# A hashed attention followed by a feed-forward layer: row maxima turned by a product with the identity, a step of the weight conversion one unit sooner, and two small groups of work moved

## The chip, the cores and the metric

The kernel runs on one core of a Trainium2 chip. The metric is device time in microseconds (us), the median of several executions. The engines are TensorE (PE, with its weight loads PEld), VectorE (DVE), ScalarE (ACT), GpSimd (POOL) and SyncE (SP), which issues nearly all DMA transfers. Times in rows of the trace count from the start of the profiled span.

## The reference

```python
B, H, S, D = q.shape                                  # 4, 8, 768, 64
q_bits = (einsum('bhsd,dk->bhsk', q, proj) > 0)       # 6 bits; k_bits likewise
q_bucket = sum(q_bits * powers, axis=-1)              # k_bucket likewise
mask = q_bucket[:, :, :, None] == k_bucket[:, :, None, :]
scores = where(mask, scale * q @ k.T, -1e9)
scores = scores - max(scores, axis=-1, keepdims=True)
attn = exp(scores)
attn = attn / (sum(attn, axis=-1, keepdims=True) + 1e-09)
attn_out = attn @ v
x = attn_out.transpose(0, 2, 1, 3).reshape(B * S, H * D)      # 3072 x 512
h = x @ w_in                                          # 512 x 2048
g = where(h >= 1, h, where(h <= -1, 0, (h + 1)**2 / 4))
out = g @ w_out                                       # 2048 x 512
```

## The kernel before, in words

All products run on fp32r operands split in a high and a low part, so that each product of the reference is three or so on PE. The first 457 us are the attention of 32 heads (four batches of eight), the rest is the feed-forward layer.

**Units.** The attention's order is written out by hand. A head has 12 units (`NU`): two halves of 384 queries by six blocks of 128 keys; unit g belongs to head g // 12. In unit g the code emits: two score products (`s_unit`, L369 and L370) into one of four PSUM buffers `s`; ACT's two exponentials (L378 writes `ph`, L383 writes the full-precision copy in place or to `pf`); for the unit before, the subtraction `pl` = full - `ph` (`lo_unit`, L39; on POOL for key blocks 0 and 3, else on DVE); then three products with V for the unit four before (`pv_unit`, L402, L404, L406) into the PSUM bank `o0` (first half of a head) or `o1` (second half). After the sixth of a half ACT copies the bank out (L412, `xs<-o`).

**Row maxima.** The maxima of a head are found two heads ahead, in six steps: two products (`max_mm`, L308) into `smax`, a pair of PSUM banks of which there is only one, and a reduction of both on DVE (`max_red`, L312, into `nm`). The six pairs stand at the end of units 4, 6, 8, 10, 12 and 14 of the head that runs, and each reduction in the unit behind; so a pair waits for the reduction of the pair before it. POOL then clamps the six columns and makes six flags (`max_clamp`, unit 15), PE turns the 128 x 12 block into rows (`max_tr`, L347, unit 17), ACT copies it to `te` (L352) and SP writes it by DMA into the row of ones of the query operand (`t<-te`, L354) and to DRAM (L355). Heads 0 to 2 do this in halves or otherwise (`row_half`, `half_put`).

**Weight conversion.** The weights come as 64-bit floats and are converted in 512-column pieces while the attention runs; each head from 3 to 26 carries one. The steps of a piece (`WeightSplit.steps`) stand at units counted from that head's first: DMA in (0), `rebias` on ACT (L66), and three on DVE: `tail` (L70, a shift right), `shifted` (L74, shift left and or) and `signed` (L78). `tail` and `shifted` write their word into PSUM bank `o0`, which is free between the copy of a head's first half (in unit 9) and the next head's first product with V in unit 16. `conv` places the steps by a list of units.

**Other tasks.** Tasks placed by `at(g, ...)` are emitted at the end of unit g, in the order of their placing. Every engine, and SP's queue, runs its instructions in the order in which they are emitted. For each pair of heads (`pr`), POOL makes the operands of the pair two ahead (`cast_h`, `low_h`), SP moves halves of them between partitions (`move`, L161, 384 KB each) and loads the raw pair after it (`load_raw`, L145). Even heads carry in addition two groups of products for the hash bits (`bits_mm`, end of units 5 and 7) with an ACT copy each (L214), and a cast of V on ACT (L287, unit 6). Once per batch `XMaker.sums_add` (L672, L673) and `sums_inv` (L677) turn the row sums into factors on DVE.

Of the kernel before, what the change touches and what calls it, by code (L numbers as in the profile page):

```python
# [11 lines left out]
F32 = mybir.dt.float32  # L12
F32R = mybir.dt.float32r
# [9 lines left out]
P = 128  # L23
NH = B * H
NPAIR = NH // 2
NJ = S // P
# [6 lines left out]
CLAMP = 2.0 ** 33  # L33
# [74 lines left out]
NU = 2 * NJ  # L108
# [3 lines left out]
def attention(ctx, tc, wst, T1, T2, qk, v, pj, cv, x_d, s_d, e_d, tasks, shared):  # L112
    nc = tc.nc
    const = ctx.enter_context(tc.tile_pool(name="aconst", bufs=1))
    work = ctx.enter_context(tc.tile_pool(name="awork", bufs=2))
    small = ctx.enter_context(tc.tile_pool(name="asmall", bufs=2))
# [6 lines left out]
    ident = const.tile([P, P], F32, name="ident")  # L123
    cvt = const.tile([32, 2], F32, name="cvt")
    cvd = const.tile([40, 2], F32, name="cvd")
    ident_r = const.tile([P, P], F32R, name="ident_r")
# [1 line left out]
    warm = const.tile([P, 2], F32, name="warm")  # L128
    nrow = [const.tile([P, NJ, 33], F32R, name=f"nrow{h}") for h in range(2)]
    pj_raw = const.tile([P, NB], F32, name="pj_raw")  # L130
    nmh = const.tile([P, 2, NJ], F32, name="nmh")
    pj_hi = const.tile([P, NB], F32R, name="pj_hi")
    pw = const.tile([P, 3, P], F32R, name="pw")
    VA = [const.tile([P, NJ, 3, D], F32R, name=f"va_{i}") for i in range(NV)]
# [157 lines left out]
    nms = {}  # L292
# [24 lines left out]
    HB = NJ // 2  # L317
# [8 lines left out]
    def half_put(hd, hf, bank):  # L326
        pr, h = hd // 2, hd % 2
        if hf == 1:
            nms.pop(hd)
        ps = obank[bank]  # L330
        nc.tensor.transpose(out=ps[0:2 * HB, 0:P], in_=nmh[:, hf], identity=ident)
        te = small.tile([2 * NJ, P], F32R, name="te")[0:2 * HB]
        nc.scalar.copy(out=te, in_=ps[0:2 * HB, 0:P])
        sl = slice(hf * HS, (hf + 1) * HS)
        nc.sync.dma_start(out=T2[pr % NQK][7:8, 0, h, sl].bitcast(F32), in_=te[0:HB].bitcast(F32))
        nc.sync.dma_start(out=e_d[hd // H][hd % H:hd % H + 1, sl], in_=te[HB:2 * HB].bitcast(F32))

    def max_clamp(hd, eng):
        nm = nms[hd]
        eng.tensor_scalar(out=nm[:, NJ:2 * NJ], in0=nm[:, 0:NJ], scalar1=CLAMP, scalar2=None,  # L340
                          op0=ALU.is_gt)
        eng.tensor_scalar(out=nm[:, 0:NJ], in0=nm[:, 0:NJ], scalar1=CLAMP, scalar2=None,
                          op0=ALU.min)

    def max_tr(hd, bank=None):
        ps = mx[hd] = ps_s.tile([P, 512], F32, name="s") if bank is None else obank[bank]
        nc.tensor.transpose(out=ps[0:2 * NJ, 0:P], in_=nms.pop(hd), identity=ident)  # L347

    def max_put(hd):
        pr, h = hd // 2, hd % 2  # L350
# [99 lines left out]
    def raw0():  # L450
        return wst.tile([P, DM, 2], I32, name="wraw").rearrange("p a b -> p (a b)").bitcast(F32)[:, 0:S].rearrange(
            "p (h s) -> p h s", h=1)

    def at(g, fn, *a):
        tasks[g].append((fn, a))

    first = [raw0(), raw0()]
# [92 lines left out]
    at(12, bits_put, 1)  # L550
    at(12, move, 1, 2)
    at(12, max_tr, 0, 0)
    at(12, max_put, 0)
    at(10, load_raw, 2)
# [4 lines left out]
    at(15, row_flags, 1)  # L559
    at(12, lambda: nc.gpsimd.memset(T2[2][0:64, 0].bitcast(F32), 0.0))  # L560
    at(17, max_tr, 1, 1)
    at(17, max_put, 1)
    at(18, half_clamp, 2, 0)
    at(19, half_put, 2, 0, 1)
    at(23, half_clamp, 2, 1)
    at(25, half_put, 2, 1, 0)
    for h, g in enumerate((20, 2 * NU + 1)):
        at(g, lambda h=h: nc.gpsimd.memset(T2[0][32:33, 0, h].bitcast(F32), 0.0))
    for hd in range(NH):
        pr, h = hd // 2, hd % 2  # L570
        g = hd * NU
        if 0 < hd < NH - 2:
            gc, gt = ((30, 32), (41, 43))[hd - 1] if hd < 3 else (g + NU + SHIFT - 1, g + NU + SHIFT + 1)
            at(gc, max_clamp, hd + 2, nc.gpsimd)
            at(gt, max_tr, hd + 2)
            at(gt, max_put, hd + 2)
        if h == 0 and pr + 2 < NPAIR:
            g0 = g + (13, 2)[pr] if pr < 2 else g
            for n in range(4):
                gq = g0 + n + (pr == 1 and n == 3)  # L580
                at(gq, cast_h, pr + 2, nc.gpsimd, n % 2, n // 2)
                at(gq, low_h, pr + 2, nc.gpsimd, n % 2, n // 2)
            for n in range(2):
                at(g0 + 3 + (pr == 1), move, pr + 2, n)
            at(g0 + 6, move, pr + 2, 2)
            if pr + 3 < NPAIR:
                at(g0 + 7, load_raw, pr + 3)
            bits_at = (((20, 1), (23, 0)), ((8, 1), (11, 0)))[pr] if pr < 2 else ((5, 1), (7, 1))
            for hf, (n, bank) in enumerate(bits_at):
                at(g + n, bits_mm, pr + 2, hf, bank)  # L590
                at(g + n + 1, bits_cmp, pr + 2, hf)
            at(g + n + 1, move, pr + 2, 3)
            at(g + n + (2 if pr else 1), bits_scale, pr + 2, nc.gpsimd if pr else nc.scalar)
            at(g + (18 if pr else 25), bits_put, pr + 2)
        if h == 0 and pr + 1 < NPAIR:
            gv = g + LAG + (2 if pr else 16)
            at(gv, cast_v, pr + 1, nc.scalar)
            at(gv + 1, split_v, pr + 1, nc.gpsimd, 0)
            at(gv + 3, split_v, pr + 1, nc.gpsimd, 1)
            if pr + 2 < NPAIR:  # L600
                at(gv + (6 if pr else 4), load_v, pr + 2)
# [6 lines left out]
    for i in range(2 * NJ):  # L608
        n = 5 * 31 + 35 * i // 4
# [495 lines left out]
def lsh_attn_ffn(ctx: ExitStack, tc: tile.TileContext, qk, v, pj, cv, w_in, w_out, out):  # L1105
    nc = tc.nc
# [16 lines left out]
    xm = XMaker(nc, x_d, s_d, er_d)  # L1123
# [25 lines left out]
    def at(g, fn, *a):  # L1149
        tasks[g].append((fn, a))  # L1150

    def conv(g, steps, offs):
        for fn, n in zip(steps, offs):
            at(g + n, fn)
# [6 lines left out]
    def wi_steps(i, cp, stage=None):  # L1161
        return ws.steps(win_v[:, :, i * P:(i + 1) * P, :], (P, NCT, P, 2), wih[i], wil[i], cp, stage, None, wq[i], word)

    def wo_steps(i, cp, stage=None, low=None):
        return ws.steps(wout_v[i], (P, DM, 2), woh[i], wol[i], cp, stage, low, None, None if stage is None else word)
# [1 line left out]
    woh = [hi for hi, lo in wo]  # L1167
    wol = [lo for hi, lo in wo]
    for i in range(NW1):
        conv((2 * i + 3) * NU, wi_steps(i, nc.scalar), (0, 9, 10, 12, 14, 17, 19, 21))  # L1170
    g0 = (NH - 4) * NU
    late = {}
    for n in range(NSTG):
        i = n - (NFT - NW1)
        stage = wq[NW1 + n] if i < 0 else xdp.tile([P, DM], F32, name=f"wd{n}")
        if i < 0:
            first, late[n] = wi_steps(NW1 + n, nc.vector, stage)
        elif i < 2:
            first, late[n] = wo_steps(i, nc.vector, stage)
        else:  # L1180
            first, late[n] = wo_steps(i, nc.scalar, stage, nc.gpsimd if i < 4 else nc.vector)
        conv((4 + 2 * n) * NU, first, (0, 9, 10, 12, 14, 16))
    for n, g in enumerate((1, 7, 13, 25, 30, 35)):
        conv(g0 + g, late[n], (0, 5, 6))

# [1 line left out]
    for b in range(B - 1):  # L1187
        g = (b + 1) * H * NU + LAG + 4
        at(g, lambda b=b: xm.sums_load(*(attn["small"].tile([P, NF], F32, name=n, bufs=1) for n in ("sm", "em")), b))
        at(g + 15, xm.sums_add)  # L1190
        at(g + 21, xm.sums_inv, b)
    gx = (NH - 2) * NU

    def load_raw():
# [16 lines left out]
    for i in (2, 3):  # L1211
        at(NH * NU + 2 * i - 10, late[i + NFT - NW1][0])
    attention(actx, tc, wst, T1, T2, qk, v, pj, cv, x_d, s_d, e_d, tasks, attn)
    actx.close()

# [5 lines left out]
    for i in range(2, NFT):  # L1221
        n = i + NFT - NW1
# [71 lines left out]
```

## Time and profile before

| | |
|---|---|
| median of 3 runs | 975.26 us (974.24 to 975.34) |
| profiled execution | 975.34 us, span 973.5 us, granted clock 1.000 |
| PE busy | 961.6 us (99%), 5050 products |
| PEld / DVE / ACT / POOL busy | 890.4 / 755.5 / 680.0 / 318.6 us |
| chain that ended last | PE 89%, DVE 4%, DMA 2%, ACT 2% |

The profiled execution is 1.84 us longer than its span; that part lies outside the first and last instruction. A busy PE means products in its pipeline: in the rows a product of 384 columns lasts 0.34 us while the next one starts 0.17 to 0.18 us behind it, so waits are read from starts and not from busy time.

### The profile page before, as it was taken

What the parts mean: (1) busy time and instruction counts of PE and PEld (TensorE: products, weight loads), DVE (VectorE), ACT (ScalarE), POOL (GpSimd) and SP (SyncE); (2) the same over time, 40 slices, a digit from 0 to 9 for tenths busy, and PEclk for the clock granted to TensorE, in tenths of its full rate; (3) what the DMA queues carried; (4) which work ended last, traced back from release to release, by engine and by line L of the source; (5) the groups of instructions that cost most, each with busy time, mean ns of one, the idle gap of its engine ahead of it and who ended that gap; (6) DMA issues with size and microseconds to landing.
All of it is one profiled execution on the core that took longest, in us unless ns stands there. A gap on an engine that the chain in (4) does not pass through costs nothing.

```text
span 973.5 us, 15576 instructions
## 1 busy us (share of the span) xinstructions
PE 961.6 (99%) x5050; PEld 890.4 (91%) x5050; DVE 755.5 (78%) x1323; ACT 680.0 (70%) x1481; POOL 318.6 (33%) x423
## 2 busy tenths in 40 slices
PE   8999999999999999999999999999999999999998
PEld 7899999999999999999989998888998888888886
DVE  8778888888888888896988787787876777655554
ACT  7889998999999998987656565455464545544444
POOL 8767776666677776466000000000000000000000
PEclk9999999999999999999999999999999999999999
DMA  5776565667666656535692578976458564454431
GB/s 163 190 185 180 150 171 167 179 181 200 183 195 168 163 158 182 142 104 147 187 337 88 158 227 287 294 245 199 120 171 230 147 182 117 148 154 119 117 90 65
DMA packets 95112, 167.55 MB, mean 172 GB/s; under 512 B 13956, under 2 KB 51960, under 8 KB 95032
## 3 DMA queue, kind: packets, MB, share of 16 engines
q1 hardware_dynamic: 94808, 166.56, 59.9%
q8 instruction: 40, 0.66, 0.3%
q14 instruction: 40, 0.33, 0.1%
q10 hardware_dynamic: 224, 0.00, 0.0%
HBM read 106.13 MB, written 33.87 MB: 144 GB/s over the span
## 4 chain that ended last, share of the span: by engine, by line
PE 89%; DVE 4%; DMA 2%; ACT 2%; issue 1%; SPq 1%; POOL 1%; DVEq 0%; ACTq 0%; POOLq 0%
PE y L828 27%; PE h L1060 18%; PE h L965 7%; PE smax L308 7%; PE o L406 6%; PE o L402 6%; PE s L370 6%; PE o L404 6%; PE s L369 6%; PE o L208 2%; DVE nm L312 2%; DVE pl L39 1%; DMA t<-te 1%; DMA t<-bits 1%; ACT ph L378 1%
## 5 line engine op out<-in xcount | busy, mean ns | idle before, releaser
L378 ACT ACTIVATE ph<-s 128x384 fp32r<-128x384 f32 x380 | 189.8, 499 | 40.1 <-PE s L370 33.9
L312 DVE TENSOR_REDUCE nm<-smax 128x1 f32<-128x768 f32 x189 | 180.0, 952 | 27.2 <-PE smax L308 26.9
L39 POOL TENSOR_TENSOR pl<-pf,ph 128x384 fp32r<-128x384 f32 x128 | 130.6, 1021 | 89.7 <-ACT pf L383 89.5
L39 DVE TENSOR_TENSOR pl<-s,ph 128x384 fp32r<-128x384 f32 x256 | 138.0, 549 | 26.0 <-ACT s L383 22.7
L793 DVE SCALAR_TENSOR_TENSOR t<-t 128x384 f32<-128x384 f32 x128 | 71.3, 557 | 106.3 <-ACT z L788 106.2
L369 PE MATMUL s<-t 128*128 128x384 f32 x384 | 131.1, 342 | 0.0
L406 PE MATMUL o<-pl,va 128*128 128x386 f32 x384 | 130.1, 339 | 0.9 <-DVE pl L39 0.9
L402 PE MATMUL o<-ph,va 128*128 128x386 f32 x384 | 130.0, 339 | 0.4 <-DVE wsq L78 0.4
L370 PE MATMUL s<-t 128*128 128x384 f32 x384 | 129.6, 337 | 0.5 <-DMA t<-te 0.5
L404 PE MATMUL o<-ph,vb 128*128 128x386 f32 x384 | 130.0, 339 | 0.0
L383 ACT ACTIVATE s<-s 128x384 f32<-128x384 f32 x252 | 126.2, 501 | 0.0
L828 PE MATMUL y<-t,ghi 128*128 128x512 f32 x384 | 124.6, 395 | 0.0
L308 PE MATMUL smax<-t 128*128 128x384 f32 x378 | 100.7, 347 | 3.6 <-DVE nm L312 2.9
L787 ACT ACTIVATE t<-h,mh 128x384 f32<-128x384 f32 x56 | 32.5, 581 | 83.3 <-PE h L965 44.1
L798 ACT CAST ghi<-z 128x384 fp32r<-128x384 f32 x129 | 65.1, 505 | 30.4 <-DVE z L794 26.6
L788 ACT ACTIVATE z<-t,m 128x384 f32<-128x384 f32 x128 | 79.0, 617 | 4.2
L828 PEld LDWEIGHTS y<-t,ghi 128*128 128x128 f32 x384 | 71.3, 188 | 11.1 <-ACT ghi L798 0.3
L1060 PE MATMUL h<-wbig,t 128*128 128x384 f32 x399 | 81.4, 336 | 0.0
L308 PEld LDWEIGHTS smax<-t 128*128 128x128 f32 x378 | 66.2, 188 | 14.9 <-DVE nm L312 13.8
L787 ACT ACTIVATE t<-wsq,mh 128x384 f32<-128x384 f32 x48 | 29.6, 617 | 67.0 <-DVE wsq L1073 40.7
L1060 PEld LDWEIGHTS h<-wbig,t 128*128 128x128 f32 x399 | 71.6, 188 | 5.3
L828 PE MATMUL y<-t,glo 128*128 128x512 f32 x192 | 76.0, 396 | 0.0
(192 smaller groups left out, 2074.2 us busy)
## 6 DMA issues: line engine op xcount, KB each, us to landing
t<-wc SPq DMA_DIRECT2D x92, 256.0 KB
t<-t SPq DMA_DIRECT2D x60, 384.0 KB
wraw<-wc SPq DMA_DIRECT2D x76, 256.0 KB
raw<-in_qk_dram SPq DMA_DIRECT2D x14, 768.0 KB
wraw<-in_w_in_dram SPq DMA_DIRECT2D x16, 512.0 KB
wraw<-in_w_out_dram SPq DMA_DIRECT2D x16, 512.0 KB
t<-ed SPq DMA_DIRECT2D x36, 192.0 KB
xd<-xs SPq DMA_DIRECT2D x32, 192.5 KB
```

The costliest lines, as they stand in the source:

```text
L39: eng.tensor_tensor(out=out, in0=a, in1=b, op=ALU.subtract)
L308: nc.tensor.matmul(out=smax[hd][:, hf, 0:HS], lhsT=t2[:, 0, h, i * P:(i + 1) * P], rhs=t2[:, 1, h, hf * HS:(hf + 1) * HS], start=True, sto ...
L312: nc.vector.tensor_reduce(out=nmp(hd)[:, i:i + 1], in_=smax[hd][:, :, 0:HS], axis=AX.XY, op=ALU.max, negate=True)
L369: nc.tensor.matmul(out=ps[:, 0:HS], lhsT=t1[:, 1, h, ks], rhs=t1[:, 0, h, sl], start=True, stop=False)
L370: nc.tensor.matmul(out=ps[:, 0:HS], lhsT=t2[:, 1, h, ks], rhs=t2[:, 0, h, sl], start=False, stop=True)
L378: nc.scalar.activation(out=ph[:, 0:HS], in_=ps[:, 0:HS], func=AF.Exp, scale=SCALE)
L383: nc.scalar.activation(out=pf, in_=ps[:, 0:HS], func=AF.Exp, scale=SCALE)
L402: nc.tensor.matmul(out=o, lhsT=wa, rhs=ph, start=(jj == 0), stop=False)
L404: nc.tensor.matmul(out=o, lhsT=wb, rhs=ph, start=False, stop=False)
L406: nc.tensor.matmul(out=o, lhsT=wa, rhs=pl, start=False, stop=(jj == NJ - 1))
L828: nc.tensor.matmul(out=ys[c][m], lhsT=g_[:, m * P:(m + 1) * P], rhs=w, start=(first and k == 0), stop=(last and k == 2))
L1060: nc.tensor.matmul(out=ps, lhsT=w[:, cs], rhs=x, start=(n == 0 and s not in (2, 3, 6)), stop=(n == 5), skip_group_check=True)
```

## The change

Five edits. (1) The block of maxima is turned by an ordinary fp32r product with the fp32r identity instead of a transposition in fp32; for that the clamped maxima go to a new fp32r tile `nmr` (and `nmh` becomes fp32r). Heads 0 and 1 keep the transposition. (2) In the lists of `conv`, `rebias` goes from unit 9 to 8 and `shifted` from 12 to 11; for the first piece `signed` goes from 14 to 13. (3) For the fourth pair of heads (`pr == 1`, pair index 3) three of the four moves go from units 30, 30, 32 to 33, 33, 34, and the load of the next raw pair from 33 to 34. (4) `sums_add` goes from 15 units behind the load to 7. (5) `sums_inv` goes from 21 units behind it to 19.

```diff
-    nmh = const.tile([P, 2, NJ], F32, name="nmh")
+    nmh = const.tile([P, 2, NJ], F32R, name="nmh")
...
-        nc.tensor.transpose(out=ps[0:2 * HB, 0:P], in_=nmh[:, hf], identity=ident)
+        nc.tensor.matmul(out=ps[0:2 * HB, 0:P], lhsT=nmh[:, hf], rhs=ident_r, start=True, stop=True)
...
     def max_clamp(hd, eng):
         nm = nms[hd]
-        eng.tensor_scalar(out=nm[:, NJ:2 * NJ], in0=nm[:, 0:NJ], scalar1=CLAMP, scalar2=None,
+        t = nms[hd] = small.tile([P, 2 * NJ], F32R, name="nmr")
+        eng.tensor_scalar(out=t[:, NJ:2 * NJ], in0=nm[:, 0:NJ], scalar1=CLAMP, scalar2=None,
                           op0=ALU.is_gt)
-        eng.tensor_scalar(out=nm[:, 0:NJ], in0=nm[:, 0:NJ], scalar1=CLAMP, scalar2=None,
+        eng.tensor_scalar(out=t[:, 0:NJ], in0=nm[:, 0:NJ], scalar1=CLAMP, scalar2=None,
                           op0=ALU.min)
 
     def max_tr(hd, bank=None):
         ps = mx[hd] = ps_s.tile([P, 512], F32, name="s") if bank is None else obank[bank]
-        nc.tensor.transpose(out=ps[0:2 * NJ, 0:P], in_=nms.pop(hd), identity=ident)
+        nm = nms.pop(hd)
+        if hd < 2:
+            nc.tensor.transpose(out=ps[0:2 * NJ, 0:P], in_=nm, identity=ident)
+        else:
+            nc.tensor.matmul(out=ps[0:2 * NJ, 0:P], lhsT=nm, rhs=ident_r, start=True, stop=True)
...
             for n in range(2):
-                at(g0 + 3 + (pr == 1), move, pr + 2, n)
-            at(g0 + 6, move, pr + 2, 2)
+                at(g0 + (7 if pr == 1 else 3), move, pr + 2, n)
+            at(g0 + (8 if pr == 1 else 6), move, pr + 2, 2)
             if pr + 3 < NPAIR:
-                at(g0 + 7, load_raw, pr + 3)
+                at(g0 + (8 if pr == 1 else 7), load_raw, pr + 3)
...
     for i in range(NW1):
-        conv((2 * i + 3) * NU, wi_steps(i, nc.scalar), (0, 9, 10, 12, 14, 17, 19, 21))
+        conv((2 * i + 3) * NU, wi_steps(i, nc.scalar), (0, 8, 10, 11, 14 - (i == 0), 17, 19, 21))
...
-        conv((4 + 2 * n) * NU, first, (0, 9, 10, 12, 14, 16))
+        conv((4 + 2 * n) * NU, first, (0, 8, 10, 11, 14, 16))
...
-        at(g + 15, xm.sums_add)
-        at(g + 21, xm.sums_inv, b)
+        at(g + 7, xm.sums_add)
+        at(g + 19, xm.sums_inv, b)
```

How the rows move is shown at three places. In the changed kernel lines below 340 keep their numbers, and those of `s_unit`, `pv_unit` and the te copies are five higher (L378 becomes L383, L383 becomes L388, L412 becomes L417, L354 becomes L359).

ACT in units 8 to 10 of an even head (head 6; `o_137` is bank `o0`), before:

```order
L378 ACTIVATE ph_161<-s 128x384
L383 ACTIVATE s<-s 128x384
L378 ACTIVATE ph_155<-s 128x384
L383 ACTIVATE pf<-s 128x384
L412 COPY xs<-o_137 128x384
L66 ACTIVATE wsq<-wraw 128x512
L378 ACTIVATE ph_156<-s 128x384
L383 ACTIVATE s<-s 128x384
```

and now:

```order
L383 ACTIVATE ph_161<-s 128x384
L388 ACTIVATE s<-s 128x384
L66 ACTIVATE wsq<-wraw 128x512
L383 ACTIVATE ph_155<-s 128x384
L388 ACTIVATE pf<-s 128x384
L417 COPY xs<-o_137 128x384
L383 ACTIVATE ph_156<-s 128x384
L388 ACTIVATE s<-s 128x384
```

`rebias` (L66) now stands ahead of unit 9's two exponentials and of the copy of bank `o0`, instead of behind them.

DVE from unit 9 of the same head to unit 2 of the next, before:

```order
L39 TENSOR_TENSOR pl_165<-s,ph_158 128x384
L70 TENSOR_SCALAR o_137<-wraw 128x512
L312 TENSOR_REDUCE nm<-smax 128x1
L39 TENSOR_TENSOR pl_167<-s,ph_160 128x384
L39 TENSOR_TENSOR pl_168<-s,ph_161 128x384
L74 SCALAR_TENSOR_TENSOR o_137<-wsq,wsc,o_137 128x512
L312 TENSOR_REDUCE nm<-smax 128x1
L39 TENSOR_TENSOR pl_163<-s,ph_156 128x384
L78 SCALAR_TENSOR_TENSOR wsq<-wsq,wsc,o_137 128x512
```

and now:

```order
L39 TENSOR_TENSOR pl_165<-s,ph_158 128x384
L70 TENSOR_SCALAR o_137<-wraw 128x512
L312 TENSOR_REDUCE nm<-smax 128x1
L39 TENSOR_TENSOR pl_167<-s,ph_160 128x384
L74 SCALAR_TENSOR_TENSOR o_137<-wsq,wsc,o_137 128x512
L39 TENSOR_TENSOR pl_168<-s,ph_161 128x384
L312 TENSOR_REDUCE nm<-smax 128x1
L39 TENSOR_TENSOR pl_163<-s,ph_156 128x384
L78 SCALAR_TENSOR_TENSOR wsq<-wsq,wsc,o_137 128x512
```

`shifted` (L74) has changed places with one subtraction; the same nine instructions stand ahead of and behind it.

SP's queue in units 30 to 36 (`t_1_78` is the operand that head 3 reads; `t_0_77` and `t_0_74` are being made for the fourth pair), before:

```order
L161 DMA t_0_77<-t_0_77 64x1536
L161 DMA t_0_74<-t_0_77 64x1536
L354 DMA t_1_78<-te 1x6x128
L355 DMA ed_67<-te 6x128
L161 DMA t_0_74<-t_0_74 64x1536
L145 DMA raw<-in_qk_dram 128x1536
L62 DMA wraw<-in_w_in_dram 128x4x256
```

and now:

```order
L359 DMA t_1_78<-te 1x6x128
L360 DMA ed_67<-te 6x128
L161 DMA t_0_77<-t_0_77 64x1536
L161 DMA t_0_74<-t_0_77 64x1536
L161 DMA t_0_74<-t_0_74 64x1536
L145 DMA raw<-in_qk_dram 128x1536
L62 DMA wraw<-in_w_in_dram 128x4x256
```

The two transfers of head 3's maxima now go ahead of the two moves.

## The prediction

> **What bounds the kernel now.** I read the page's busy times first, then the instructions of the maxima products with what they wait for, then single units of the attention engine by engine in the timeline.
>
> ```profile
> PE 961.6 (99%) x5050; PEld 890.4 (91%) x5050; DVE 755.5 (78%) x1323; ACT 680.0 (70%) x1481; POOL 318.6 (33%) x423
> ```
>
> ```profile
>   DVE nm L312: 16.7, 48
> ```
>
> PE is the bound over the whole span, so an edit is worth what it adds to or takes from PE's waits. The second row is from the view of line L308: PE and its weight loads sat idle 16.7 us, 48 times, ahead of a maxima product, for the reduction of the pair before it. No other releaser comes near it in the attention, and nothing in the diff touches the feed-forward part. So the question is what the edits do to that wait. On PE it looks so (a pair at the end of unit 0, then the pair of unit 2 with the product ahead of it, in head 9; then the pair of unit 2 behind the last conversion):
>
> ```profile
> 145.72 0.51 PE L308 MATMUL smax<-t 128*128 128x384 f32 x2
> ...
> 147.65 0.34 PE L406 MATMUL o<-pl,va 128*128 128x386 f32 x1
> 148.02 0.62 PE L308 MATMUL smax<-t 128*128 128x384 f32 x2
> ...
> 395.38 0.62 PE L308 MATMUL smax<-t 128*128 128x384 f32 x2
> ```
>
> An undisturbed pair takes 0.51 and starts 0.17 behind the product ahead (the steps between neighbours). At 148.02 it starts 0.37 behind and takes 0.62: a wait of 0.20 + 0.11 = 0.31 us. Behind the last piece, at 395.38, the pair takes 0.62 again. The 24 conversion pieces (heads 3 to 26) each leave one such wait in unit 2 of the next head. They come in two kinds, by whether the head that carries the piece is even or odd.
>
> **Even heads: ACT is full.** ACT, then DVE, in head 8:
>
> ```profile
> 142.09 0.49 ACT L383 ACTIVATE s<-s 128x384 f32<-128x384 f32 x1
> 142.50 0.49 ACT L378 ACTIVATE ph<-s 128x384 fp32r<-128x384 f32 x1
> ...
> 143.23 0.49 ACT L412 COPY xs<-o 128x384 f32<-128x384 f32 x1
> 143.59 0.71 ACT L66 ACTIVATE wsq<-wraw 128x512 f32<-128x512 f32 x1
> 144.17 0.51 ACT L378 ACTIVATE ph<-s 128x384 fp32r<-128x384 f32 x1
> ```
>
> ```profile
> 143.75 0.69 DVE L70 TENSOR_SCALAR o<-wraw 128x512 int32<-128x512 int32 x1
> 144.36 0.95 DVE L312 TENSOR_REDUCE nm<-smax 128x1 f32<-128x768 f32 x1
> 145.22 1.21 DVE L39 TENSOR_TENSOR pl<-s,ph 128x384 fp32r<-128x384 f32 x2
> 146.35 0.74 DVE L74 SCALAR_TENSOR_TENSOR o<-wsq,wsc,o 128x512 int32<-128x512 int32 x1
> 147.01 0.95 DVE L312 TENSOR_REDUCE nm<-smax 128x1 f32<-128x768 f32 x1
> 147.88 0.55 DVE L39 TENSOR_TENSOR pl<-s,ph 128x384 fp32r<-128x384 f32 x1
> 148.34 0.74 DVE L78 SCALAR_TENSOR_TENSOR wsq<-wsq,wsc,o 128x512 int32<-128x512 int32 x1
> ```
>
> ACT has no gap: each instruction starts before the row ahead has ended. The copy ends at 143.23 + 0.49 = 143.72 and `tail` (L70), which writes the bank that was copied, starts at 143.75. So `tail` is tied to the copy. The reduction at 147.01 ends at 147.96, and the pair of maxima starts 0.17 later.
>
> The edit puts `rebias` ahead of unit 9's exponentials and of that copy. Steps from the rows: behind L383 at 142.09 it starts 0.36 later (as 143.23 to 143.59), and the exponential 0.58 behind it (143.59 to 144.17): 143.03 instead of 142.50. The copy is late by 0.53 and `tail` starts at 144.28. From there DVE goes without a gap: reduction +0.61 (143.75 to 144.36), subtraction +0.86 (144.36 to 145.22), `shifted` +0.46 (as 147.88 to 148.34), subtraction +0.66 (146.35 to 147.01), reduction +0.46: 147.33 instead of 147.01. What it wins back of the 0.53 is the gap ahead of the second subtraction, which today waits for its exponential (two of them take 1.13 to the start of L74 where 2 x 0.46 would do) and which `shifted` now fills. Loss: 0.32 us a head. Part of it will show one pair sooner: the reduction ahead ends at 144.36 + 0.53 + 0.95 = 145.84, the pair can start at 146.01 and wanted 145.72. That 0.29 is not to be added; the wait of unit 2 shrinks by it, because DVE's row of work is not pushed by PE there. Twelve even heads (4, 6 ... 26): **+3.84 us**. Bounds: 0.53 each (nothing won back, +6.4), and a gain of 0.21 each, the whole gap won and no delay (-2.5). I take the middle value because every step in it is from a row of this stretch.
>
> **Odd heads: ACT has a gap.** Head 7, ACT, DVE and PE:
>
> ```profile
> 127.21 0.49 ACT L383 ACTIVATE s<-s 128x384 f32<-128x384 f32 x1
> 128.05 0.49 ACT L378 ACTIVATE ph<-s 128x384 fp32r<-128x384 f32 x1 [0.35 <-PE s L370]
> ```
>
> ```profile
> 129.33 0.70 DVE L70 TENSOR_SCALAR o<-wraw 128x512 int32<-128x512 int32 x1 [0.21 <-ACT xs L412]
> ...
> 132.58 0.95 DVE L312 TENSOR_REDUCE nm<-smax 128x1 f32<-128x768 f32 x1
> ```
>
> ```profile
> 133.32 0.34 PE L406 MATMUL o<-pl,va 128*128 128x386 f32 x1
> 133.59 0.62 PE L308 MATMUL smax<-t 128*128 128x384 f32 x2
> ```
>
> Here ACT waits 0.35 for PE ahead of unit 9's exponential. `rebias` falls into that gap: 127.21 + 0.36 + 0.58 = 128.15 instead of 128.05, so copy and `tail` are 0.10 late. The same chain from `tail` at 129.43 gives the reduction at 132.48 instead of 132.58. The wait of 0.10 + 0.11 = 0.21 falls by 0.10. Eight such heads (5, 7, 11, 13, 15, 19, 21, 23): **-0.8 us**; bounds 0 and -1.7 (the whole wait).
>
> **Sums of a batch.** The other odd heads, 9, 17 and 25, carry `sums_add` in the same row of DVE work:
>
> ```profile
> 156.74 0.69 DVE L70 TENSOR_SCALAR o<-wraw 128x512 int32<-128x512 int32 x1 [0.21 <-ACT xs L412]
> ...
> 158.67 0.37 DVE L672 SCALAR_TENSOR_TENSOR sm<-em,sm 128x48 f32<-128x48 f32 x1
> ...
> 160.31 0.95 DVE L312 TENSOR_REDUCE nm<-smax 128x1 f32<-128x768 f32 x1
> ```
>
> Without it, with `tail` at 156.84 and the same 3.05 of steps, the reduction comes at 159.89 instead of 160.31. That is 0.42 a head, three heads: **-1.26 us**. It now stands in unit 3 of a head, where the next reduction comes two units later, and the reciprocal too. The cover is DVE's wait for PE, seen in the reductions' group:
>
> ```profile
> L312 DVE TENSOR_REDUCE nm<-smax 128x1 f32<-128x768 f32 x189 | 180.0, 952 | 27.2 <-PE smax L308 26.9
> ```
>
> DVE idles 27.2 us ahead of 189 reductions, 0.14 each and none at units 0 and 2 in the rows above, so more elsewhere. Were that cover gone, the sums (0.52 today, 0.42 + 0.10) and a reciprocal of an estimated like size would give back up to 3 x 2 x 0.5 = 3 us; I keep this as the far end. The sums must also have landed seven units behind their load, instead of 15.
>
> **The fourth pair's moves.** In unit 36 PE waits for head 3's row of maxima. SP, ACT, then PE:
>
> ```profile
> 56.63 1.16 SPq L161 DMA_DIRECT2D t<-t  x2
> 57.88 1.21 SPq L354 DMA_DIRECT2D t<-te  x1
> ```
>
> ```profile
> 57.31 0.25 ACT L352 CAST te<-s 12x128 fp32r<-12x128 f32 x1
> ```
>
> ```profile
> 61.50 0.33 PE L369 MATMUL s<-t 128*128 128x384 f32 x1
> 62.30 0.44 PE L370 MATMUL s<-t 128*128 128x384 f32 x1 [0.47 <-DMA t<-te]
> ```
>
> The row is ready at 57.56, is issued at 57.88 behind two moves of 384 KB, and L370 starts 0.80 behind L369 instead of 0.17, and takes 0.44 instead of 0.34: 0.73 us lost. With the moves behind it the row goes first: **-0.73 us**, bounds 0 and -0.73. What is queued behind it is the moves, the raw load and the first weights: they come about 1 us later, and are wanted by PE, POOL and ACT from unit 44 on.
>
> The first piece (head 3) trades one wait for another: PE waits at
>
> ```profile
> 80.50 0.41 PE L402 MATMUL o<-ph,va 128*128 128x386 f32 x1 [0.37 <-DVE wsq L78]
> ```
>
> for `signed`, which now comes a reduction sooner, while `shifted` (0.66 of DVE) now stands ahead of the reduction that the last maxima pair of that head waits for. I count 0, from -0.5 to +0.5.
>
> **Product for transposition.** A transposition and an fp32r product of the same 128 columns (three in a row), each ahead of the score products:
>
> ```profile
> 124.07 0.27 PE L347 MATMUL s<-ident,nm 128*12 128x128 f32 x1
> 124.10 0.42 PE L369 MATMUL s<-t 128*128 128x384 f32 x1
> 124.36 0.34 PE L370 MATMUL s<-t 128*128 128x384 f32 x1
> ```
>
> ```profile
> 24.08 0.34 PE L258 MATMUL smax<-ident_r,nrow 128*33 128x128 f32 x3
> 24.26 0.39 PE L369 MATMUL s<-t 128*128 128x384 f32 x1
> 24.48 0.34 PE L370 MATMUL s<-t 128*128 128x384 f32 x1
> ```
>
> From the transposition's start to L370's it is 0.03 + 0.26 = 0.29 us; from the last of the three products 0.06 + 0.22 = 0.28. Both are some 0.11 over the 0.17 of a lone step, so the kind of product is not what costs. There are 31 (29 heads and two halves): at most 0.3 us, I take **-0.1**. The Trainium skill ("TensorE: Matmul & The Clock Gate", "LDWEIGHTS (loading the stationary operand)") gives a weight load as its columns over 1.2, 107 ns for 128. By that rule the excess is the next load, which a product this short cannot hide, and the trace's 0.11 agrees. The two clamps on POOL stay two and have two units to the product.
>
> **The sum.** 3.84 - 0.8 - 1.26 - 0.73 - 0.1 = +0.95. Against the profiled execution, 975.34 us (its span of 973.5 and 1.84 around it, 0.08 over the median of 975.26), this is 976.3 us. A measurement of this kernel can tell about 0.2%, 1.95 us, from no change: so 973.3 to 977.2 counts as the same.
>
> **Rivals.**
> - *Slower: the late copy costs in full.* In even heads the 0.53 reaches the reduction undiminished, because the second subtraction still waits for its exponential. 12 x 0.53 = 6.4, less 2.9 of the other terms: 978.8. It decides from 0.40 us a head on ((1.95 + 2.89) / 12). For it: ACT's rows have no gap. Against it: unit 10's and 11's exponentials are not moved later, and DVE reaches the subtraction later. Chance 0.28, with the smaller sizes beyond 977.2.
> - *Faster: the copy is not delayed,* and every head wins the gap on DVE: 12 x 0.21 and 8 x 0.2 off, sums 1.5, moves 0.7: 6.3 less, 969.0. It decides if the even heads lose under 0.08 each ((2.89 - 1.95) / 12). For it: only rounding of steps of ACT's stands between. Against it: ACT's order is fixed and full there. Chance 0.22, with the part gains up to 973.3.
> - *The transposition's whole length is on the path.* 0.27 against some 0.22 for the other (0.34 for three that start 0.06 apart), 31 times: 1.5 less, 974.9, still the same. The Trainium skill, section "Part 4: PE-mode transpose" of that page, reads so: about 275 ns each, and not counted as PE being busy. The length agrees with 0.27, but L369 starts 0.03 behind it and the clock stays at 1.000. Chance 0.05, within the next.
>
> **How the numbers follow.** Same, with the sum above: 0.50; slower 0.28; faster 0.22. The likeliest is 976.3, its own range 974.9 to 977.2 (odd heads and head 3 at their lower ends; above, where the case ends). For 8 in 10 the range goes down to 970.5, which leaves out the full gain of every head (1 in 10), and up to 979.0, just over the slower rival (1 in 10).
>
> **What would show it.** In the profile after, even heads should have `tail` some 0.5 us behind where it stood against the product ahead, a wait of about 0.3 at unit 0 that is not there now and about 0.3 at unit 2 still; odd heads 0.1 at unit 2; the large waits of heads 10, 18 and 26 and that of unit 36 gone; the L308 waits for L312 up by about 1 to 2 us in all. The forecast is wrong if `tail` in even heads starts as early as before, if the wait at unit 2 does not shrink by what unit 0 shows, or if a new wait for a DMA appears at unit 44 to 48 or 111.

## The result and the profile after

| | before | after |
|---|---|---|
| median of 6 runs each | 975.12 us (973.94 to 976.60) | 980.16 us (979.36 to 980.82) |
| ratio, 95% interval | | 1.0052 (1.0040 to 1.0063) |
| profiled execution / span | 975.34 / 973.5 us | 980.79 / 979.0 us |
| granted clock | 1.000 | 0.998 |

The change makes the kernel 5.0 us slower. The forecast was 976.3, so the same, with a range up to 979.0: wrong.

The page's busy times, after:

```profile
PE 965.4 (99%) x5050; PEld 891.9 (91%) x5050; DVE 754.6 (77%) x1323; ACT 680.8 (70%) x1481; POOL 317.8 (32%) x423
```

The view of line L308, PE's and PEld's idle time ahead of a maxima product and its cause:

```profile
  DVE nm L312: 18.2, 54
```

That is 1.5 us more than the 16.7 before, inside the "1 to 2" that the prediction gave, and far from 5. The rest is found by cutting both traces at the start of each unit's first score product (us; unit 383 is the last):

| units | before | after | difference |
|---|---|---|---|
| 0 to 30 | 41.01 | 40.99 | 0 |
| 30 to 36 | 8.28 | 9.59 | +1.31 |
| 36 to 48 | 13.83 | 13.09 | -0.74 |
| 48 to 60 | 14.84 | 18.17 | +3.33 |
| 60 to 324 | 302.07 | 304.15 | +2.08 |
| 324 to 383 | 61.89 | 61.39 | -0.50 |

The largest entry is head 4 (units 48 to 59). PE at its start, in the timeline (start, length, instruction, idle time and its releaser), before and then after:

```profile
75.33 0.34 PE L369 MATMUL s<-t 128*128 128x384 f32 x1
75.51 0.33 PE L370 MATMUL s<-t 128*128 128x384 f32 x1
```

```profile
75.91 0.34 PE L374 MATMUL s<-t 128*128 128x384 f32 x1
78.45 0.44 PE L375 MATMUL s<-t 128*128 128x384 f32 x1 [2.20 <-DMA t<-te]
...
79.35 0.53 PE L409 MATMUL o<-ph,vb 128*128 128x386 f32 x1
79.67 0.52 PE L411 MATMUL o<-pl,va 128*128 128x386 f32 x1
```

After the change the second score product of unit 48 waits for head 4's row of maxima: 2.36 us lost (2.54 from L374 to L375 instead of 0.17). From 79.1 the products last 0.52 instead of 0.34 and start 0.32 apart instead of 0.175. A table of stretches says why (stretch, its length, busy time and instructions of PE, PEld, DVE, ACT and POOL, then PE's granted clock, DMA share, GB/s):

```profile
72.30:75.70 3.40, 3.40 (x21) 3.40 (x20) 2.63 (x4) 2.53 (x6) 0.15 (x1) 1.00 0.98 203
75.70:79.10 3.40, 1.20 (x8) 0.88 (x7) 2.51 (x5) 1.88 (x6) 2.30 (x3) 1.00 0.31 83
79.10:82.50 3.40, 3.40 (x12) 3.40 (x11) 2.17 (x3) 1.60 (x5) 2.54 (x4) 0.50 0.38 131
```

After the stretch with the wait the clock was granted at 0.50 for 3.4 us: 12 products instead of 21, another 9 x 0.175 = 1.6 us. Together that is some 4.0; 3.33 are left in the table because the 0.7 us of waits that these units had before, for the first piece, fall away behind it.

Where the row was in the meantime is seen on ACT, which copies it, and in SP's queue:

```profile
71.84 0.25 ACT L357 CAST te<-s 12x128 fp32r<-12x128 f32 x1
```

```profile
58.86 0.74 SPq L359 DMA_DIRECT2D t<-te  x1
...
60.22 2.46 SPq L161 DMA_DIRECT2D t<-t  x3
...
67.66 0.47 SPq L161 DMA_DIRECT2D t<-t  x1
...
70.78 3.88 SPq L280 DMA_DIRECT2D t<-bits  x4
76.09 0.75 SPq L359 DMA_DIRECT2D t<-te  x1
```

It is ready at 72.09 and issued at 76.09. Before, the first move was issued at 56.63; now SP stands at head 3's row until 58.86, and the moves follow at 60.22, 3.6 us later. Before, head 4's row was issued at:

```profile
72.33 0.74 SPq L354 DMA_DIRECT2D t<-te  x1
```

Everything between has kept its order behind the moves, and is late with them. The queue's waits from 70 to 80 us name two of the causes (total, times, longest):

```profile
SPq L359 <- DMA t<-t: 1.4, 1, 1.4
SPq L280 <- DMA wraw<-in_w_in_dram: 1.1, 1, 1.1
```

The transfers of the bits stand ahead of the row and wait for the weights to land; the row then waits for a move to land, to whose data it has no relation. The program shows the reason: SP's transfers take eight completion semaphores in turn, and each waits until the one eight places ahead has landed. The row is number 58, the last move number 50:

```
50 L161 DMA t_0_74<-t_0_77 64x1536 [waits DMAHW3_49,DMAHW6_49,DMAHW1_49,PE_49]
58 L359 DMA t_2_79<-te 1x6x128 [waits DMAHW6_49,Activation_49]
```

That the DMA engines were idle until the moves came is in the DMA view from 54 to 80 us (busy tenths in 40 slices of 0.65 us; before, then after):

```profile
DMA  3920049899709996898989998999731047950000
```

```profile
DMA  3920000000079969999897978999989887310268
```

From 56 to 61 us less than a tenth is busy after the change, and the backlog ends some 3 us later.

The attention's other heads went as the prediction had them. Head 8 on ACT, DVE and PE:

```profile
146.94 0.65 ACT L66 ACTIVATE wsq<-wraw 128x512 f32<-128x512 f32 x1
...
148.23 0.48 ACT L417 COPY xs<-o 128x384 f32<-128x384 f32 x1
```

```profile
148.74 0.69 DVE L70 TENSOR_SCALAR o<-wraw 128x512 int32<-128x512 int32 x1 [0.69 <-ACT xs L417]
```

```profile
150.00 0.34 PE L411 MATMUL o<-pl,va 128*128 128x386 f32 x1
150.35 0.62 PE L308 MATMUL smax<-t 128*128 128x384 f32 x2
...
152.39 0.34 PE L411 MATMUL o<-pl,va 128*128 128x386 f32 x1
152.80 0.62 PE L308 MATMUL smax<-t 128*128 128x384 f32 x2
```

The copy (L417) ends at 148.71, and `tail` (L70) starts 1.26 ahead of unit 0's L411 where it was 1.80 ahead: 0.54 late, with an idle DVE ahead of it. The pair of unit 0 now waits (0.35 - 0.17) + 0.11 = 0.29, that of unit 2 0.24 + 0.11 = 0.35. Behind odd head 7, and behind head 9 with its sums:

```profile
137.89 0.34 PE L411 MATMUL o<-pl,va 128*128 128x386 f32 x1
138.06 0.60 PE L308 MATMUL smax<-t 128*128 128x384 f32 x2
```

```profile
165.53 0.33 PE L411 MATMUL o<-pl,va 128*128 128x386 f32 x1
165.74 0.62 PE L308 MATMUL smax<-t 128*128 128x384 f32 x2
```

0.09 and 0.15 are left of the 0.21 and 0.55 before (for head 9's sums, L406 at 160.70 and a pair of 0.62 at 161.31).

### The profile page after: what moved, and what is told of

It reads as the page before. It is cut to its first block, busy times and chain, and to the rows that moved or that the text cites. A ratio compares the mean times of both kernels' runs of the same rounds, so it can differ in the third digit from the quotient of the medians.

```text
span 979.0 us, 15556 instructions
## 1 busy us (share of the span) xinstructions
PE 965.4 (99%) x5050; PEld 891.9 (91%) x5050; DVE 754.6 (77%) x1323; ACT 680.8 (70%) x1481; POOL 317.8 (32%) x423
## 4 chain that ended last, share of the span: by engine, by line
PE 83%; DVE 8%; ACT 5%; issue 2%; DMA 2%; POOL 0%; DVEq 0%; ACTq 0%
PE y L833 27%; PE h L1065 18%; PE h L970 7%; PE smax L308 6%; PE s L375 5%; PE s L374 5%; PE o L411 5%; PE o L407 5%; PE o L409 5%; DVE nm L312 3%; DVE pl L39 2%; PE o L208 2%; ACT ph L383 2%; DVE o L70 1%; DMA t<-te 1%
## 5 line engine op out<-in xcount | busy, mean ns | idle before, releaser
L383 ACT ACTIVATE ph<-s 128x384 fp32r<-128x384 f32 x380 | 189.3, 498 | 44.2 <-PE s L375 39.8
L375 PE MATMUL s<-t 128*128 128x384 f32 x384 | 130.0, 339 | 3.7 <-DMA t<-te 3.7
L374 PE MATMUL s<-t 128*128 128x384 f32 x384 | 131.0, 341 | 0.0
L411 PE MATMUL o<-pl,va 128*128 128x386 f32 x384 | 130.4, 340 | 0.4 <-DVE pl L39 0.4
L388 ACT ACTIVATE s<-s 128x384 f32<-128x384 f32 x252 | 125.8, 499 | 0.0
L308 PE MATMUL smax<-t 128*128 128x384 f32 x378 | 102.1, 351 | 3.6 <-DVE nm L312 2.2
L308 PEld LDWEIGHTS smax<-t 128*128 128x128 f32 x378 | 65.5, 189 | 17.7 <-DVE nm L312 16.0
L375 PEld LDWEIGHTS s<-t 128*128 128x128 f32 x384 | 72.7, 189 | 4.5 <-DMA t<-te 4.3
```

What stands on the lines that cost most here:

```text
L308: nc.tensor.matmul(out=smax[hd][:, hf, 0:HS], lhsT=t2[:, 0, h, i * P:(i + 1) * P], rhs=t2[:, 1, h, hf * HS:(hf + 1) * HS], start=True, sto ...
L374: nc.tensor.matmul(out=ps[:, 0:HS], lhsT=t1[:, 1, h, ks], rhs=t1[:, 0, h, sl], start=True, stop=False)
L375: nc.tensor.matmul(out=ps[:, 0:HS], lhsT=t2[:, 1, h, ks], rhs=t2[:, 0, h, sl], start=False, stop=True)
L383: nc.scalar.activation(out=ph[:, 0:HS], in_=ps[:, 0:HS], func=AF.Exp, scale=SCALE)
L388: nc.scalar.activation(out=pf, in_=ps[:, 0:HS], func=AF.Exp, scale=SCALE)
L411: nc.tensor.matmul(out=o, lhsT=wa, rhs=pl, start=False, stop=(jj == NJ - 1))
```

## The experiments

Theory Q: the late moves hold up head 4's row, and the wait and the half clock cost some 3 us. Theory R: all of the loss comes from `rebias` one unit sooner. S: where `rebias` stands does not matter, only the place of `shifted` does. T: the transposition lay on PE's path; U: the product in its place makes head 2's row late. Each comparison has its own runs of the kernel before beside it (single ones took 973.6 to 978.7 us), so ratios are compared; a ratio can differ by 0.001 to 0.002 from the quotient of the two medians. "Half clock" below counts the runs with a mean granted clock of 0.998 or less, which is what one stretch of 3.4 us at 0.50 makes of it.

### The moves back

```diff
-                at(g0 + (7 if pr == 1 else 3), move, pr + 2, n)
-            at(g0 + (8 if pr == 1 else 6), move, pr + 2, 2)
+                at(g0 + 3 + (pr == 1), move, pr + 2, n)
+            at(g0 + 6, move, pr + 2, 2)
...
-                at(g0 + (8 if pr == 1 else 7), load_raw, pr + 3)
+                at(g0 + 7, load_raw, pr + 3)
```

> The changed kernel with the fourth pair's moves and the raw load back at units 30, 30, 32 and 33. Theory Q (the moves, put behind head 3's row, start 3 us late, so that head 4's row lands late, PE waits 2.2 us in unit 48 and then runs 3.4 us at half clock): the wait of unit 48 and the half clock go, the 0.73 us of unit 36 come back; 980.2 - 3.3 + 0.7 = 977.6 us, granted clock 1.000. Theory R (all of the loss is rebias ahead of the copy in even heads): no change, 980 us. If the 1.5 us wait of unit 30 also belongs to the moves: 976.3. If it belongs to edit 1 or to chance, it may stay.

978.89 us, ratio 1.0020 (1.0008 to 1.0031), against 1.0052 with the late moves: the edit costs about 3 us by the ratios (1.3 by the bare medians; units 48 to 60 of the two traces differ by 3.35). Those units take 14.82 us, there is no wait for a row at unit 48, and 2 of 10 runs have the half clock where all 6 after had it. Q holds in what it says of unit 48, though its total of 977.6 does not quite. Some 2 us of loss are left for R. One thing goes against the prediction's gain: the trace shows no wait at unit 36 either (36 to 48: 13.10), although the moves stand ahead of head 3's row again. That wait comes and goes.

### `rebias` back in unit 9

```diff
-(0, 8, 10, 11, 14 - (i == 0), 17, 19, 21))
+(0, 9, 10, 11, 14 - (i == 0), 17, 19, 21))
...
-(0, 8, 10, 11, 14, 16))
+(0, 9, 10, 11, 14, 16))
```

> The changed kernel with rebias back in unit 9, shifted kept in unit 11. Theory Q and my step for even heads (tail 0.53 late with rebias ahead of the copy): the waits of units 0 and 2 behind the twelve even heads (0.28 and 0.34 us in the trace) shrink to 0.1 in unit 2, those behind odd heads to nearly nothing; 980.2 - 12 x 0.53 - 11 x 0.1 = 972.7 us, with the half clock at unit 48 still there (clock 0.998). Theory R: back to before or better by the same, 972 to 975, and the clock at 1.000. Rival S (where rebias stands does not matter, shifted does): 980, waits of units 0 and 2 as they are.

972.96 us, ratio 0.9966 (0.9951 to 0.9981): this kernel is faster than the one before. `tail` on DVE, and the pairs of units 0 and 2 on PE, behind head 8:

```profile
144.55 0.69 DVE L70 TENSOR_SCALAR o<-wraw 128x512 int32<-128x512 int32 x1 [0.15 <-ACT xs L417]
```

```profile
146.37 0.34 PE L411 MATMUL o<-pl,va 128*128 128x386 f32 x1
146.54 0.51 PE L308 MATMUL smax<-t 128*128 128x384 f32 x2
...
148.47 0.34 PE L411 MATMUL o<-pl,va 128*128 128x386 f32 x1
148.65 0.57 PE L308 MATMUL smax<-t 128*128 128x384 f32 x2
```

`tail` stands 1.82 ahead of its product again, and both waits are gone but for 0.06. Units 84 to 324 take 270.29 us (after 276.48, before 274.70): the prediction's rival "the copy is not delayed" as it was worked out, 0.2 us a head. Against leaving it in unit 9, `rebias` in unit 8 costs 8 us by the ratios, by undoing the gain of `shifted` and adding a loss. S falls. The late moves still show: 7 of 10 runs have the half clock, and the profiled execution waits 2.51 us at unit 48, without it.

### Both back

Both diffs above together.

> The changed kernel with the moves back and rebias back in unit 9; left of the change are the product with the identity, shifted in unit 11, signed of the first piece in unit 13, and the sums. If the two causes are separate they add: 980.2 - 2.6 - 7.5 = 970.1 us, clock 1.000, faster than both kernels. If the moves' loss only hides behind another wait, the two together give less than their sum: 972 to 974.

971.16 us, ratio 0.9936 (0.9915 to 0.9957). The same step from the kernel with only the moves back, 0.0084, as between the two others, 0.0086: the moves and `rebias` act apart from each other. In this trace PE loses 0.7 us at unit 48 to head 4's row although the moves are back; the waits for the first piece shrink by as much behind it (48 to 60: 14.86); so with early moves that wait is small, but not always nothing. One wait of 0.3 us is left in head 17, where the sums, now seven units behind their load, take 0.96 instead of 0.37 on DVE:

```profile
259.79 0.96 DVE L677 SCALAR_TENSOR_TENSOR sm<-em,sm 128x48 f32<-128x48 f32 x1
```

### The transposition back

```diff
-        if hd < 2:
-            nc.tensor.transpose(out=ps[0:2 * NJ, 0:P], in_=nm, identity=ident)
-        else:
-            nc.tensor.matmul(out=ps[0:2 * NJ, 0:P], lhsT=nm, rhs=ident_r, start=True, stop=True)
+        nc.tensor.transpose(out=ps[0:2 * NJ, 0:P], in_=nm, identity=ident)
```

(and the tiles in fp32 again, and a transposition in `half_put` too)

> The changed kernel with the fp32 transpositions and the old tile of maxima back (edit 1 undone alone). My step: within 0.3 us of the changed kernel, 979.9 to 980.5. Rival T (the transposition's 0.27 us against 0.22 is on PE's path, 31 times): 1.5 us slower, 981.7. Rival U (the new tile or the product delays the row of head 2 and makes the wait of unit 30): 1.3 us faster, 978.9, and no wait for the row in unit 30.

980.37 us, ratio 1.0041 (1.0027 to 1.0056): no difference from the change as a whole that can be told. The groups of the two, the product in the kernel after and the transposition in this one (count, then shortest, median and longest in ns):

```profile
L352 PE MATMUL s<-ident_r,nmr x29: 220/222/227, 58.3 to 443.7; 128*12 128x128 f32 x29
```

```profile
L349 PE MATMUL s<-ident,nm x29: 270/273/275, 56.9 to 441.8; 128*12 128x128 f32 x29
```

It is 51 ns shorter and saves nothing: units 84 to 324 take 276.43 us with the transposition and 276.48 with the product. T falls. U is not borne out either: this trace has no wait in unit 30 (30 to 36: 8.27), but neither have those of the moves back and of `rebias` back, which keep the product, while the next run keeps the transposition and has it (9.52). 6 of 10 runs here have the half clock.

### The late moves alone

The kernel before with edit (3) only, the first diff turned round.

> The kernel before with edit 3 alone (three moves and the raw load of the fourth pair later). Theory Q: head 3's row is in time (0.7 us won at unit 36), the moves start 3 us late, head 4's row comes late: a wait of 2.1 to 2.6 us at unit 48, of which 0.7 replaces the first piece's wait at unit 52; 976.6 us, or 978.3 where the half clock follows. Theory R (the loss is rebias alone): 974.6 us, the 0.7 of unit 36 won and nothing at unit 48.

978.43 us, ratio 1.0024 (1.0014 to 1.0034). The step that the prediction priced at -0.73 costs 2.3 us by itself, and 7 of 10 runs have the half clock. PE at unit 48, and the two stretches from 77.74 on:

```profile
76.31 0.34 PE L369 MATMUL s<-t 128*128 128x384 f32 x1
79.69 0.44 PE L370 MATMUL s<-t 128*128 128x384 f32 x1 [3.04 <-DMA t<-te]
```

```profile
77.74:81.15 3.41, 1.46 (x8) 1.46 (x9) 0.70 (x2) 0.87 (x2) 0.03 (x1) 1.00 0.37 100
81.15:84.56 3.41, 3.41 (x13) 3.41 (x12) 2.40 (x4) 1.74 (x4) 3.25 (x5) 0.50 0.17 61
```

### The early `rebias` alone

The kernel before with 9 turned to 8 in both lists.

> The kernel before with rebias in unit 8 instead of 9 and shifted left in unit 12. My step by step chain: tail comes 0.53 late behind even heads whatever shifted does, and the gap ahead of the second subtraction closes by that alone, so even heads lose 0.32 us each as in the changed kernel, with a wait at unit 0: 975.3 + 3.8 - 0.8 = 978.3 us. Rival (the loss in even heads needs shifted in unit 11): 975, no wait at unit 0.

978.81 us, ratio 1.0034 (1.0022 to 1.0046), no wait at unit 48, all ten clocks at 0.999 or more. From one head's start to the next, PE takes 0.36 us longer behind even heads on the mean and 0.09 less behind odd ones. With `shifted` early as well (the kernel after) it is 0.36 and 0.09: with the late copy, `shifted` in its new place brings nothing.

### The early `shifted` alone

The kernel before with 12 turned to 11 (and 14 to 13 for the first piece).

> The kernel before with shifted alone moved from unit 12 to 11 (and signed of the first piece from 14 to 13). The gap of 0.21 us ahead of the second subtraction is filled and nothing is delayed: 0.2 us less behind each of 23 pieces (the wait there is 0.2 to 0.3), 970.7 us. Rival (DVE is simply full there, order does not matter): 975.3.

972.55 us, ratio 0.9967 (0.9953 to 0.9981). The early `shifted` gains alone, but 3.2 us and not the 4.6 expected: on the mean 0.23 behind even heads, and only 0.08 behind odd ones.

### Products that fill the wait

The change as it is, with 14 products of a tile of zeros (128 x 256) ahead of unit 48's scores, in the bank that the scores then overwrite. They keep PE busy during the wait, and nothing else.

```diff
+        if g == 48:
+            for _ in range(14):
+                keep_busy(ps)
```

> The changed kernel with 14 products on zeros (128x256) at the start of unit 48, into the buffer that the unit's scores overwrite, so that PE works through 1.6 us of the wait for head 4's row. Theory Q: the row lands when it did, the wait left is under 1 us, the clock stays at 1.000 and the twelve or so products that ran at half clock take 1.7 us less: 978.4. Rival (the products at half clock were slow for the same reason as the late row, not for the idle time): they stay slow, 980.

979.67 us, ratio 1.0039 (1.0026 to 1.0053): the total can't tell the two expectations apart. The rows can:

```profile
75.52 1.84 PE L431 MATMUL s<-idle 128*128 128x256 f32 x14
77.20 0.34 PE L377 MATMUL s<-t 128*128 128x384 f32 x1
79.08 0.44 PE L378 MATMUL s<-t 128*128 128x384 f32 x1 [1.54 <-DMA t<-te]
...
79.71 0.34 PE L410 MATMUL o<-ph,va 128*128 128x386 f32 x1
```

The row comes no sooner: counted from unit 36 it is 1.0 us later than in the kernel after, and the wait left is 1.54, not under 1. But the products behind it run at full rate, and 1 of 9 runs has the half clock where all 6 after had it: it was PE's idle time that made them slow, not what made the row late. The 14 products stand ahead of unit 48's first score product and so count in units 36 to 48 (14.77 instead of 13.09); units 48 to 60 take 15.96 instead of 18.17. Units 36 to 60 together take 30.73 instead of 31.26: the later row takes back most of what the clock gave.

### Head 4's row ahead of the bits

The change as it is, with the fourth pair's transfers of hash bits in unit 44 instead of 42, so that the row stands ahead of them in SP's queue.

```diff
-            at(g + (18 if pr else 25), bits_put, pr + 2)
+            at(g + (25, 20)[pr] if pr < 2 else g + 18, bits_put, pr + 2)
```

> The changed kernel with one thing moved: the four transfers of the fourth pair's hash bits (L280) go from unit 42 to unit 44, so that head 4's row of maxima stands ahead of them in SP's queue; the moves stay as late as the change has them. In the changed kernel's trace that row is copied at 71.84 to 72.09 and issued only at 76.09: SP first issues the four bits transfers (70.78 to 74.66), then waits 1.4 for a move to land. Theory Q (the wait at unit 48 comes from SP's queue: the bits ahead of the row, and the landing of the move eight places ahead of it): the row is issued at about 72.5, the wait of 2.2 at unit 48 is gone and the half clock with it, units 48 to 60 take about 14.9 instead of 18.17, the kernel some 3.3 less: 976.5 to 978. Rival B (the row is late because some 1 MB of moves, V and outputs is ahead of it on the DMA engines, wherever it stands in the queue): it lands at 77 to 78 as before, a wait of 1 to 2 at unit 48 stays, 979 to 980.

977.56 us, ratio 1.0019 (1.0008 to 1.0029), level with the moves put back (1.0020); no run has the half clock. The time is as Q said. The profiled execution, at 979.64 the slowest of the ten, shows that B is not wrong either. SP, then PE:

```profile
71.80 0.79 SPq L359 DMA_DIRECT2D t<-te  x1
...
73.19 4.67 SPq L280 DMA_DIRECT2D t<-bits  x4
```

```profile
75.59 0.34 PE L374 MATMUL s<-t 128*128 128x384 f32 x1
77.98 0.44 PE L375 MATMUL s<-t 128*128 128x384 f32 x1 [2.06 <-DMA t<-te]
```

The row is issued 4.3 us sooner and PE still waits 2.06 for it here. In the packet records ten of the twelve packets of 512 B that belong to the row and its copy to DRAM had ended by 75.18, the last two at 77.26. In the kernel after all twelve ended 1.4 to 1.9 us behind the issue at 76.09. So SP's queue held the row in the kernel after; with that taken away, its transfer could still end late, and here two of its packets, or of the copy's, did. The Trainium skill ("DMA: Bandwidth & Descriptors", "Queues, rings and completion order") says that each DMA engine takes its descriptors in order and that a completion lands only after the earlier writes of that engine. The two late packets would fit that, but it is not shown: which engines they were on, the trace doesn't tell.

### Two versions that beat both kernels

The first: both edits back, head 3's and head 4's rows issued from ACT's queue instead of SP's, and the sums nine units behind their load.

```diff
+            q = nc.scalar if hd in (3, 4) else nc.sync
...
-        at(g + 7, xm.sums_add)
+        at(g + 9, xm.sums_add)
```

> The kernel with moves and rebias back in their old units, and two edits more: the maxima rows of heads 3 and 4 are written by a DMA that ACT issues instead of SP, and the sums of a batch stand nine units behind their load instead of seven. Theory Q: rows no longer queue behind moves on SP's ring, so units 36 and 48 have no wait for them in any run (0 to 1.6 us with the moves back) and the 0.3 us of head 17's unit 6 go: 969.5 to 970.5 against 971.2. Rival (the rows are late because all transfers share the 16 engines, whoever issues them): the waits at 36 and 48 stay, 971; and if ACT's issue takes as long as SP's 0.7 to 1.2 us, exponentials behind it come late.

969.69 us, ratio 0.9943 (0.9929 to 0.9957). ACT issues head 4's row at 71.06, right behind its copy, and nothing waits at unit 48; the wait in head 17 is gone. At unit 36, 0.3 us are still lost to head 3's row (61.81 for L376 behind 61.44 for L375), so the expectation of no wait there did not hold.

The second: late moves, `rebias` back in unit 9, the row ahead of the bits, the sums at nine units.

> The changed kernel with rebias back in unit 9, the bits transfers of the fourth pair in unit 44 as in the run beside this one, and the sums nine units behind their load instead of seven; the late moves stay. Theory Q: the kernel with rebias back alone took 972.96 and lost 1.9 or more between units 48 and 60; without that, and with 0.3 for the sums of head 17, 969 to 970.5, level with the best version so far (969.7), and units 36 to 48 keep their 13.09. Rival B: the wait at unit 48 stays, 972 to 973.

970.40 us, ratio 0.9945 (0.9930 to 0.9960): level with the first. In its trace the wait at unit 48 is down to 0.8 us, not gone, and most of it is won back from the waits for the first piece (48 to 60: 15.00). This execution, the slowest of six, met another wait, in unit 30 for the second half of head 2's row, and the half clock behind it:

```profile
53.09 0.34 PE L374 MATMUL s<-t 128*128 128x384 f32 x1
55.46 0.45 PE L375 MATMUL s<-t 128*128 128x384 f32 x1 [2.03 <-DMA t<-te]
```

```profile
53.22:56.63 3.41, 1.38 (x8) 1.10 (x7) 1.42 (x2) 0.75 (x3) 3.33 (x5) 1.00 0.42 93
56.63:60.05 3.42, 3.42 (x12) 3.42 (x12) 1.52 (x2) 2.62 (x6) 3.25 (x7) 0.50 0.00 0
```

## Why the prediction was wrong

**The step that failed is "The fourth pair's moves: -0.73 us".** Its sentence "they come about 1 us later, and are wanted by PE, POOL and ACT from unit 44 on" has two faults. The moves come 3.6 us later in the profiled execution (2.2 where the wait at unit 30 is absent, as in the transposition's run, with the row issued at 57.50 and the moves at 58.86), because SP now stands idle at a row that isn't ready while the moves could have gone. And the list of what is wanted stops at the moves, the raw load and the weights. The next row of maxima in the same queue, head 4's, is wanted at unit 48. The working asked what stands behind the moved transfers by size and not by who waits for it. A new wait for a DMA at unit 44 to 48 was named as what would make the forecast wrong, without a price or a chance. Measured: 0.74 won at unit 36 in the two traces, 3.33 lost between units 48 and 60; by itself the step costs 2.3 us (moves alone), by difference 3.1 (moves back).

**The win at unit 36 was read from one execution.** With the early moves in place that wait cost 0 (moves back, early `rebias` alone), 0.3 (best version, where ACT issues the row) or 1.5 us (both back, early `shifted` alone). With the late moves it is 0 in all seven traces. So the step does win there, but -0.73 was one draw from 0 to 1.5.

**The half clock** was no term of the sum. It is 1.6 of the some 4.0 us at unit 48.

**The terms of the attention's heads held.** Behind even heads +0.36 us (+0.32 forecast; 12 steps add 4.34, forecast 3.84), behind odd ones -0.09 (-0.10; 8 steps, -0.69 for -0.8), behind the sums -0.41 (-0.42; -1.22 for -1.26). The size of the wait at unit 0, that of unit 2, the 0.5 of `tail` and the sum of the waits at L308 came out as written. So the rival "late copy in full", with 0.53 a head, is out, and so, for this kernel, is "not delayed". One reason did not hold: the prediction wins part of the 0.53 back because `shifted` fills a gap on DVE. With `rebias` early and `shifted` in its old unit the loss is the same 0.36, and the two subtractions start 0.47 apart behind head 8: DVE's being late closes the gap by itself.

**The first piece**, counted as 0, is 0: head 4's twelve units take 14.84 before, 14.82 with the moves back. **The product for the transposition** is 0 where -0.1 was taken; its wording "so the kind of product is not what costs" is shown.

The forecast of +0.95 with 3.33 for the missed wait and 0.75 for the small misses of the heads and the product gives 5.0, as measured. That it fits so closely is partly luck: in the two profiled executions, 5.45 apart, two further differences nearly cancel: +1.31 at unit 30 (the second half of head 2's row, late also in runs without the late moves or without the early `rebias`) and -1.06 in head 30. They differ between executions of kernels that don't touch them, and what decides them stays open.

## What to carry to other kernels

A transfer that is moved behind another inherits the time at which that one becomes ready, and so does all that is queued behind it: follow the queue to the next small transfer that someone waits for, however far down it stands. Two edits of one list are priced apart: here the early `shifted` was worth -3.2 us, and the early `rebias`, which made the copy ahead of `tail` late, took it back and 3 us more. A wait that one trace shows for a DMA is one draw; look at several executions before its removal goes into a sum.

## What the runs showed of the hardware

**The clock falls in fixed stretches.** In each trace clock changes lie on a grid of 3.413 us. What goes with a fall is PE's busy time within one stretch of that grid. Inside the kernel, the stretches with 1.20 (after), 1.38 (second version), 1.46 (moves alone) and 1.66 us (transposition back) busy were each followed by one at 0.50; none with 1.87 or more was. It is not the gap's length: `rebias` back waited 2.51 us at unit 48 across two stretches, busy for 2.00 in one and 2.48 in the next, and lost no clock. The stretch of 1.87 in the row-first run, and the one with the last products of the kernel before:

```profile
74.05:77.46 3.41, 1.87 (x11) 1.55 (x9) 2.52 (x5) 3.35 (x8) 1.77 (x3) 1.00 0.37 120
```

```profile
968.24:971.65 3.41, 1.60 (x7) 0.94 (x5) 0.69 (x1) 1.31 (x3) 0.00 (x0) 1.00 0.98 363
```

The second was not followed by a fall, with 1.60 busy, less than the 1.66 that was. So no sharp threshold in busy time is shown; it lies somewhere near half of a stretch. The Trainium skill ("TensorE: Matmul & The Clock Gate", "Part 1: The HAM clock gate (the "warmup" mystery)") has the free-running window of 3413 ns and the halving, and the traces agree; it speaks of a whole idle window before the clock falls, and here some 1.75 us idle in one (3.41 less 1.66) were enough. By that rule the wait at unit 48 would have cost 2.4 us and no more.

**A small transfer may be late in two ways**: by the eight completion semaphores that SP's transfers take in turn (the row stood 1.4 us at a move that it has nothing to do with), and, once issued, in its last packets (5.5 us from issue to the last of them in the row-first run, at most 1.9 in the kernel after). That other transfers held these packets is likely, and not shown.
